# A fused attention and two-layer-pair kernel: the last product's first four row chunks in the seven-product form, the other two added plain

## The chip, the cores and the metric

The kernel runs on one core of one Trainium2 chip. The metric is device time in microseconds (us) of one execution; lower is better. The engines are TensorE (PE, with its weight loads shown as PEld), VectorE (DVE), ScalarE (ACT), GpSimd (POOL) and SyncE (SP), which issues all DMAs here.

## The reference

Linear attention with a normalised output, a softplus layer pair, and a max-of-three layer pair, all in float32:

```python
kv = einsum('bhsd,bhse->bhde', k, v); out = einsum('bhsd,bhde->bhse', q, kv)
x = (out / sqrt(mean(out*out, -1) + 1e-6) * g_norm)      # 4608 tokens x 512
g = softplus(x @ w_in)                                   # 512 -> 2048
x = g @ w_out                                            # 2048 -> 512
h = maximum(maximum(x @ w1, x @ w2), x @ w3)             # 512 -> 768
y = h @ w2_out                                           # 768 -> 512
```

## The kernel before

The 4608 tokens are worked in five passes of two halves each (464 tokens to a half, 448 in the last pass). Activations lie with features on the partitions, so a feature dimension is counted in row chunks of 128.

**The seven-product form.** A product of a 2x2 block of weights with a 2x2 block of activations (two row chunks by two token halves) is done with seven block products and some sums instead of eight block products (Winograd's form of Strassen's method). `run_group` issues the seven in the order 1, 5, 6, 2, 7, 4, 3 at the places of `SLOT`; `combine` (or `combine32` in pass 0) makes the seven sums of activations, `sums_of_weights` those of the weights, and products accumulate in three kinds of PSUM bank (`BANK`: X and Y with two buffers, W with one). After products 1, 6 and 7 the bank is copied out, because later products go on adding to it. The products x @ w_in (8 groups, "H"), g @ w_out (8, "X") and x @ w1..w3 (9, "2") have this form; the last, h @ w2_out, has not: `out_part` runs it as 6 row chunks by 4 output chunks by 2 halves.

**Precision.** In pass 0 a block is one float32 matmul (`L318`, `L696`; two instructions each). In the passes 1 to 4 each operand is split into a high and a low part of the type float32r, and a block is three matmuls (`mm3`, L127 to L129). A split is a cast on ACT (L111) and a subtraction on POOL or DVE (L117).

**Weights.** In pass 0 the raw weights are loaded, converted (`to_f32`), summed and, for groups below `LATE` = 19, split into four units per group (`make_unit`), which are kept in DRAM for the later passes (`keep`). For the groups from 19 on, and for the last product's weights ("oa" for row chunks 0 to 3, "ob" for 4 and 5), only the float32 sums are kept; pass 1 loads them (`load_sums`, tile `st`, two buffers), splits and keeps them (`make_later`). The passes 2 to 4 load ready units (`load_unit`). Three units of a group hold two blocks (tile `u`, four buffers, or `ux`); the fourth, for product 3, holds one (tile `u3`, `U3_BUFS` = 2), and so do the "ob" units.

**Order.** Every step is entered with `at(t, ...)`, t being counted in places of one block product (six matmuls in passes 1 to 4). The steps are issued in order of t, and the framework's scheduler then orders each engine's instructions by this priority among those that it holds ready, gives out the tile buffers as they come free, and adds all waits. On the chip each engine runs its list in order. `attention_beside` puts the next pass's attention (`load_kv`, `kv_mm`, `kv_evict`, `out_mm`) beside the end of a pass, and from pass 2 on `start["H0"]` lies `SHARED` = 12 places before the pass's base, so that its first group overlaps the last product of the pass before. The group 16 begins at `base2`, the last product at `base3 = base2 + 63`.

Of the kernel before, what the change touches and what calls it, by code (L numbers as in the profile page):

```python
# [15 lines left out]
P = 128  # L16
# [16 lines left out]
LATE = 19  # L33
# [7 lines left out]
def kernel(  # L41
# [157 lines left out]
    def raw_of(g):  # L199
        if g < 8:  # L200
            return [w_in[2 * g + i] for i in range(2)]
        if g < 16:
            return [w_out[2 * (g - 8) + i] for i in range(2)]
        f, j = divmod(g - 16, 3)
        return [w123[2 * f + i, j] for i in range(2)]
# [61 lines left out]
    def convert_out(j, i):  # L267

        if i == 0:
            sw["o", j] = pools["raw"].tile([P, 3, 512], F32, tag="sw", bufs=3, name="swo")  # L270
        to_f32(raws.pop(("o", j, i)), sw["o", j][:, i])
# [288 lines left out]
    def run_pass(pas, base):  # L560
# [5 lines left out]
        def weights_at(t, g, stretch=1):  # L566
            if pas == 0:
# [83 lines left out]
        def h2_done(fp, j, w, src):  # L651
# [9 lines left out]
            if j == 2:  # L661
                src = mx.pop(key)
                at_ = 2 * fp + w // 20, w % 10 - 1
                if pas == 0:
                    hh[at_] = src
                else:
                    hi, lo = gc_tile("hh", N, F32R), gc_tile("hl", N, F32R)
                    split(nc.scalar, src, hi, lo, nc.gpsimd)
                    hh[at_] = (hi, lo)

# [9 lines left out]
        if pas + 1 < NPASS:  # L680
            attention_beside(pas + 1, start["X30"], base2)
# [4 lines left out]
        acc = {}  # L686

        def out_part(e, t, part):
            if part == 0:
                acc[e, t] = psum("at" if e > 1 else ("at", "X")[e], "oacc")[:, 0:N]  # L690
            if pas == 0:
                w = sw["o", e // 2][:, 2 * part or e % 2]
                for k in range((4, 2)[part]):
                    f = 4 * part + k
                    o = k + (part and 2 * (e % 2))
                    nc.tensor.matmul(acc[e, t], w[:, o * P:(o + 1) * P], hh[f, t], start=f == 0,  # L696
                                     stop=f == NF2 - 1)
            else:
                u = units[pas, (("oa", "ob")[part], e)]
            for k in range(0 if pas == 0 else (4, 2)[part]):  # L700
                f = 4 * part + k
                xh, xl = hh[f, t]
                cs = slice(k * P, (k + 1) * P)
                if part == 0:
                    wh, wl = u[:, 0, cs], u[:, 1, cs]
                else:
                    wh, wl = u[:, 0, cs], u[:, 0, slice(256 + k * P, 256 + (k + 1) * P)]
                mm3(acc[e, t], wh, wl, xh, xl, f == 0, f == NF2 - 1)
            if part == 1:
                o = ctile("osb", N)  # L710
                if t:
                    nc.vector.tensor_copy(o, acc[e, t])
                else:
                    nc.scalar.copy(o, acc[e, t])
                a = TOK[pas] + t * N
                nc.sync.dma_start(out=out[e * P:(e + 1) * P, a:a + N], in_=o)

        t = base3 + 2.05
        if pas == 0:
            for j in range(2):  # L720
                tj = t + 12 * j
                for i in range(3):
                    src = w2_out[2 * j + i if i < 2 else KC + j]
                    jobs.append((tj - 12 + 2 * i, ("o", j, i), src, convert_out, (j, i)))
                at(tj + 1, keep_sums, ("o", j))
        parts = [(e, part) for part in range(2) for e in range(2)]
        parts += [(e, part) for e in (2, 3) for part in range(2)]
        for i, (e, part) in enumerate(parts):
            if pas == 1:
                c0, n = ((512 * (e % 2), 512), (1024 + 256 * (e % 2), 256))[part]  # L730
                make_later(t, (("oa", "ob")[part], e), 2 - part, ("o", e // 2), c0, n)
            elif pas:
                own = i == 0
                at(t - (6 if own else LEAD), load_unit, pas, (("oa", "ob")[part], e), 2 - part, own)
            for h in range(2):
                at(t, out_part, e, h, part)
                t += (2, 1)[part] * (1 if i < 4 or pas in (0, NPASS - 1) else 1.6)
        if 0 < pas < NPASS - 1:
            t -= 7.2
        return t - 0.05  # L740
# [57 lines left out]
def _laid_out(inputs):  # L798
# [10 lines left out]
    def cols(w):  # L809
# [9 lines left out]
        [w2[:, :, 0:4].reshape(KC, P, DM),  # L819
# [39 lines left out]
```

## Time and profile before

| | us |
|---|---|
| median of 3 runs | 1489.62 (1486.07 to 1490.92) |
| the profiled execution, its own time | 1490.04 |
| its span in the profile | 1488.2 |
| PE, PEld busy | 1427.3, 1129.2 |
| DVE, ACT, POOL busy | 933.3, 834.5, 674.9 |

The span runs from the first to the last instruction; 1.8 us of the execution's time lie outside it. Busy times of the engines overlap each other. A matmul's busy time is modelled and longer than its place in the stream (0.37 us for a 464-column one that follows the one before after 0.21 us), so idle time before an instruction says more than the busy share.

### The profile page before, as it was taken

The page shows a single profiled execution, that of the slowest core. Times are in us where ns is not written, and L with a number is a line of the kernel's source. Part 1 is how long each engine was busy: PE and PEld are TensorE (multiplying, and loading weights), DVE is VectorE, ACT ScalarE, POOL GpSimd, SP SyncE. Part 2 cuts the span into 40 slices and gives each one's busy share as a digit, 9 for nine tenths or more (in the row PEclk, how much of TensorE's full clock was granted, in tenths as well). Part 3 has the DMA queues.
Part 4 walks back from the last instruction along what each step waited for, and adds up shares of the span by engine and source line. Part 5 has one row for each costly group of instructions (what it writes and reads, how often), then busy time and mean ns, then how long its engine had stood idle before and what let it go on. Part 6 is the DMA issues. An engine that isn't in the chain of part 4 may idle for free.

```text
span 1488.2 us, 18882 instructions
## 1 busy us (share of the span) xinstructions
PE 1427.3 (96%) x6164; PEld 1129.2 (76%) x6164; DVE 933.3 (63%) x1476; ACT 834.5 (56%) x1625; POOL 674.9 (45%) x613
## 2 busy tenths in 40 slices
PE   6898999999999999999999999999999999999999
PEld 4344444555588888778889898888888888898898
DVE  5787887689365676773666556355675554567432
ACT  5676453564197636764866366387636636864321
POOL 3587776643243454451545434434444452534311
PEclk9999999999999999999999999999999999999999
DMA  7657667964366775766566676566665656666572
GB/s 271 250 196 271 213 222 275 324 205 152 120 200 202 220 243 198 263 218 217 186 216 218 228 259 195 168 197 213 217 213 191 201 179 206 203 219 211 188 220 97
DMA packets 107954, 315.56 MB, mean 212 GB/s; under 512 B 12113, under 2 KB 23633, under 8 KB 107857
## 3 DMA queue, kind: packets, MB, share of 16 engines
q1 hardware_dynamic: 107856, 314.36, 63.8%
q8 instruction: 50, 0.82, 0.2%
q14 instruction: 48, 0.39, 0.1%
HBM read 248.78 MB, written 65.54 MB: 211 GB/s over the span
## 4 chain that ended last, share of the span: by engine, by line
PE 72%; DVE 9%; ACT 8%; DMA 4%; issue 4%; POOL 3%; SPq 0%; ACTq 0%; POOLq 0%; DVEq 0%
PE Xo L128 3%; PE Xo L127 3%; PE Xo L318 3%; PE Xo L129 3%; PE Xx L127 3%; PE Xx L129 3%; PE Xx L128 3%; PE Xh L127 3%; PE Xh L129 3%; PE Xh L128 3%; PE oacc L129 3%; PE oacc L128 3%; PE oacc L127 3%; PE oacc L696 3%; PE kvps L412 2%
## 5 line engine op out<-in xcount | busy, mean ns | idle before, releaser
L117 POOL TENSOR_TENSOR lo<-e,hi 128x464 fp32r<-128x464 f32 (+1 forms) x160 | 190.6, 1224 | 201.3 <-ACT hi L111 165.2
L123 POOL TENSOR_TENSOR e<-e 128x464 f32<-128x464 f32 (+1 forms) x40 | 48.2, 1204 | 190.1 <-DVE t L123 172.6
L111 ACT COPY m<-Xo 128x464 f32<-128x464 f32 (+1 forms) x135 | 72.6, 542 | 88.8 <-PE Xo L129 76.9
L117 POOL TENSOR_TENSOR hl<-m,hh 128x464 fp32r<-128x464 f32 (+1 forms) x48 | 58.5, 1222 | 106.2 <-ACT hh L111 106.2
L111 ACT CAST hi<-e 128x464 fp32r<-128x464 f32 (+1 forms) x160 | 87.5, 576 | 21.7 <-PE Yx L128 17.5
L111 ACT CAST hi<-t 128x464 fp32r<-128x464 f32 (+1 forms) x96 | 52.0, 543 | 84.5 <-DVE e L123 38.2
L375 DVE SCALAR_TENSOR_TENSOR e<-h,e 128x464 f32<-128x464 f32 (+1 forms) x80 | 69.5, 871 | 47.1 <-ACT e L374 46.5
L120 DVE TENSOR_TENSOR x<-x,Xx 128x464 f32<-128x464 f32 (+1 forms) x120 | 75.2, 628 | 31.5 <-PE Xx L129 30.1
L374 ACT ACTIVATE e<-e 128x464 f32<-128x464 f32 (+1 forms) x160 | 92.8, 588 | 2.7
L373 ACT ACTIVATE e<-e 128x464 f32<-128x464 f32 (+1 forms) x160 | 92.8, 588 | 2.4
L117 POOL TENSOR_TENSOR u<-sw,u 128x512 fp32r<-128x512 f32 (+1 forms) x76 | 87.9, 1186 | 10.4 <-ACT u L111 10.4
L127 PE MATMUL Xo<-hi,u 128*128 128x464 f32 (+1 forms) x228 | 87.9, 385 | 3.9 <-ACT m L111 3.6
L128 PE MATMUL Xo<-lo,u 128*128 128x464 f32 (+1 forms) x228 | 86.6, 380 | 0.2 <-DVE lo L117 0.2
L220 ACT ACTIVATE cv<-raw 128x512 f32<-128x512 f32 x56 | 35.8, 640 | 90.2 <-DVE sw L231 49.3
L129 PE MATMUL Xo<-hi,u 128*128 128x464 f32 (+1 forms) x228 | 86.1, 378 | 0.0
L123 POOL TENSOR_TENSOR sw<-sw 128x256 f32<-128x256 f32 x75 | 57.1, 762 | 62.0 <-DVE sw L231 45.2
L519 POOL TENSOR_TENSOR og<-og,r 128x464 f32<-128x464 f32 (+1 forms) x32 | 41.0, 1280 | 90.1 <-DVE r L509 82.0
L127 PE MATMUL Xh<-hi,u 128*128 128x464 f32 (+1 forms) x194 | 73.3, 378 | 4.7 <-ACT h L111 4.3
L129 PE MATMUL Xh<-hi,u 128*128 128x464 f32 (+1 forms) x194 | 71.9, 371 | 0.0
L127 PE MATMUL Xx<-hi,u 128*128 128x464 f32 (+1 forms) x192 | 71.8, 374 | 0.0
L128 PE MATMUL Xh<-lo,u 128*128 128x464 f32 (+1 forms) x194 | 71.8, 370 | 0.0
L111 ACT COPY h<-Xh 128x464 f32<-128x464 f32 (+1 forms) x108 | 57.6, 536 | 25.0 <-PE Xh L129 21.4
(229 smaller groups left out, 4330.3 us busy)
## 6 DMA issues: line engine op xcount, KB each, us to landing
u<-wd SPq DMA_DIRECT2D x198, 512.0 KB, 4.3
ux<-wd SPq DMA_DIRECT2D x96, 512.0 KB, 3.4
wd<-u SPq DMA_DIRECT2D x79, 512.0 KB, 3.0
u<-wd SPq DMA_DIRECT2D x106, 256.0 KB, 3.7
raw<-in_w_out_dram SPq DMA_DIRECT2D x22, 512.0 KB, 4.2
k<-in_kp_dram SPq DMA_DIRECT2D x32, 320.0 KB, 5.0
v<-in_vp_dram SPq DMA_DIRECT2D x32, 320.0 KB, 5.3
raw<-in_w_dram SPq DMA_DIRECT2D x18, 512.0 KB, 3.9
```

The lines of the kernel that those rows point to most:

```text
L111: nc.scalar.copy(hi, src)
L117: eng_lo.tensor_tensor(out=lo, in0=src, in1=hi.bitcast(F32), op=ALU.subtract)
L120: eng.tensor_tensor(out=o, in0=a, in1=b, op=ALU.add)
L123: eng.tensor_tensor(out=o, in0=a, in1=b, op=ALU.subtract)
L127: nc.tensor.matmul(acc, wh, xh, start=first, stop=False, skip_group_check=on)
L128: nc.tensor.matmul(acc, wh, xl, start=False, stop=False, skip_group_check=on)
L129: nc.tensor.matmul(acc, wl, xh, start=False, stop=last, skip_group_check=on)
L318: nc.tensor.matmul(acc, w[:, c * P:(c + 1) * P], rhs[m, c], start=first and c == 0, stop=c == 1, skip_group_check=not first)
L373: nc.scalar.activation(e, e, AF.Exp, scale=-1.0)
L374: nc.scalar.activation(e, e, AF.Ln, bias=1.0)
L375: nc.vector.scalar_tensor_tensor(out=e, in0=src, scalar=0.0, in1=e, op0=ALU.max, op1=ALU.add)
L696: nc.tensor.matmul(acc[e, t], w[:, o * P:(o + 1) * P], hh[f, t], start=f == 0, stop=f == NF2 - 1)
```

## The change

The row chunks 0 to 3 of h become two groups more (25 and 26, one for two output chunks each) in the seven-product form; their activations' sums are made by `combine_h` in the middle of the "2" groups. The row chunks 4 and 5 are added plain (`rest`) into the same banks before these are read out; for the fourth block, 22, into a bank of its own. `LATE` is no longer a bound but a list of ten groups that are spread over the X groups, the "2" groups and the new ones; the subtraction of every other unit made in pass 1 goes to POOL instead of DVE. The next pass's first kv products move from the middle of the X groups (X30) to six places before `base2`, two places apart instead of three. The last product is counted with 24 places, of which two are waiting.

```diff
-LATE = 19
+LATE = (9, 11, 13, 15, 17, 19, 21, 23, 25, 26)
...
     def split_unit(key, size):
         u = units[1, key] = unit_tile(size, 1)
         src = st.pop(key)
-        if key[0] == "oa":
-            split(nc.scalar, src, u[:, 0], u[:, 1], nc.vector)
-        else:
-            split(nc.scalar, src.rearrange("p (i n) -> p i n", i=size), u[:, :, 0:256], u[:, :, 256:512], nc.vector)
+        split(nc.scalar, src.rearrange("p (i n) -> p i n", i=size), u[:, :, 0:256], u[:, :, 256:512],
+              nc.gpsimd if key[1] % 2 else nc.vector)
...
-    def attention_beside(pas, t_kv, t0):
+    def attention_beside(pas, t0):
...
-        for t, tt in ((0, t_kv), (1, t0 + 16)):
+        for t, tt, d in ((0, t0 - 6, 2), (1, t0 + 16, 3)):
...
-                    at(tt + 3 * p - (10 if p < 2 else 5.85), load_kv, b, p)
-                    at(tt + 3 * p + 0.1, kv_mm, b, p)
-                at(tt + (9.2 if t == 0 else 10.35), kv_evict, b)
+                    at(tt + d * p - (10 if p < 2 else 2 * d - 0.15), load_kv, b, p)
+                    at(tt + d * p + 0.1, kv_mm, b, p)
+                at(tt + 3 * d + (0.2 if t == 0 else 1.35), kv_evict, b)
...
-                if g >= LATE:
+                if g in LATE:
                     at(t + 1, keep_sums, g)
-                for k in range(4 if g < LATE else 0):
+                for k in range(0 if g in LATE else 4):
                     at(t + 1.6 * k, make_unit, g, k)
-            elif pas == 1 and g >= LATE:
+            elif pas == 1 and g in LATE:
...
-            if j == 2:
+            if j == 2 and fp == 2:
...
-                    hi, lo = gc_tile("hh", N, F32R), gc_tile("hl", N, F32R)
+                    hi, lo = ge_tile(pas, "hh", N).bitcast(F32R), ge_tile(pas, "hl", N).bitcast(F32R)
                     split(nc.scalar, src, hi, lo, nc.gpsimd)
...
+        def combine_h(c, steps):
+            tiles = [mx[c, w] for w in TILES]
+            if pas == 0:
+                combine32(gc_tile, ho, c, tiles)
+            else:
+                combine(gc_tile, ho, c, tiles, steps, "W")
+
+        for c in range(2):
+            for s in range(6 if pas else 1):
+                at(base2 + 21 * c + 28 + 1.2 * s, combine_h, c, (s,))
...
-            attention_beside(pas + 1, start["X30"], base2)
+            attention_beside(pas + 1, base2)
...
+        def rest(E, i, t, acc, first=False):
+            e = 2 * E + i
+            for k in range(2):
+                if pas == 0:
+                    o = (2 * i + k) * P
+                    nc.tensor.matmul(acc, sw["o"][:, E, o:o + P], hh[k, t], start=first and k == 0,
+                                     stop=k == 1, skip_group_check=not first)
                 else:
+                    u = units[pas, ("ob", e)][:, 0]
+                    mm3(acc, u[:, k * P:(k + 1) * P], u[:, 256 + k * P:256 + (k + 1) * P], *hh[k, t],
+                        first and k == 0, k == 1, not first)
+
+        def last_group(E, t0, stretch):
...
+            def after(m, b):
+                bank.update(b)
+                if m in (1, 6, 7):
+                    w = {1: 11, 6: 12, 7: 22}[m]
+                    c[w] = ctile(f"o{w}", N)
+                    nc.scalar.copy(c[w], b["X"])
+                if m == 7:
+                    add(nc.vector, c[22], c[22], b["Y"])
+
+            def finish(w):
+                i, t = w // 20, w % 10 - 1
+                acc = psum("at", "oacc")[:, 0:N] if w == 22 else bank[{11: "W", 21: "X", 12: "Y"}[w]]
+                rest(E, i, t, acc, w == 22)
+                if w == 21:
+                    c[21] = ctile("o21", N)
+                    nc.scalar.copy(c[21], acc)
                 else:
+                    add(nc.vector, c[w], c[w], acc)
+                store(i, t, c[w])
+
+            weights_at(t0, 25 + E, stretch)
+            run_group(t0, pas, 25 + E, ho, after, stretch)
+            for w, m, d in ((11, 2, 2.5), (21, 4, 0.5), (12, 3, 0.4), (22, 3, 0.8)):
+                at(t0 + stretch * SLOT[m] + d, finish, w)
+            for i in range(2):
+                key = ("ob", 2 * E + i)
+                t = t0 + stretch * SLOT[2] + 2.5 + 2 * i
+                if pas == 1:
+                    make_later(t, key, 1, "o", 512 * E + 256 * i, 256)
+                elif pas:
+                    at(t - LEAD, load_unit, pas, key, 1)
...
+        last_group(0, base3, 1.25)
+        last_group(1, base3 + 9, 1.25)
+        return base3 + 24
```

The removed function `out_part` and its calls are in the kernel above.

## Rows read from the trace of the kernel before

**Rows 1.** The profile page: span, busy time (share) and instructions of each engine.
```profile
span 1488.2 us, 18882 instructions
PE 1427.3 (96%) x6164; PEld 1129.2 (76%) x6164; DVE 933.3 (63%) x1476; ACT 834.5 (56%) x1625; POOL 674.9 (45%) x613
```

**Rows 2.** Windows: busy us per engine by stretch, granted clock, DMA share, GB/s; five passes.
```profile
0.00:404.00 404.00, 367.34 (x1063) 188.60 (x1064) 304.22 (x478) 211.53 (x411) 233.38 (x249) 0.98 0.65 226
404.00:680.00 276.00, 265.71 (x1253) 231.81 (x1252) 184.61 (x282) 175.43 (x343) 121.21 (x98) 0.99 0.68 223
680.00:956.00 276.00, 272.94 (x1338) 242.04 (x1337) 157.74 (x252) 163.10 (x315) 119.39 (x98) 0.99 0.65 211
956.00:1232.00 276.00, 272.81 (x1310) 241.37 (x1309) 157.32 (x252) 161.90 (x315) 119.05 (x98) 0.99 0.62 200
1232.00:1488.00 256.00, 248.47 (x1208) 225.35 (x1206) 129.39 (x213) 122.55 (x242) 81.88 (x70) 1.00 0.61 192
```

**Rows 3.** Chain that ended last, start and us: matmuls of passes 0, 1 and 4.
```profile
372.54 31.13 PE oacc L696 x80
...
406.39 0.21 PE Xh L128
...
1471.12 0.20 PE oacc L127
```

**Rows 4.** Waits of PE: total us, times, longest; the ones that bear on this.
```profile
PE Xx L318 <- DVE x L120: 5.7, 4, 1.9
PE Xo L127 <- ACT hi L111: 5.7, 4, 1.8
PE Xo L127 <- ACT m L111: 3.6, 2, 3.2
PE Yo L127 <- DVE m L660: 2.2, 3, 1.4
PE Xo L128 <- DVE lo L117: 2.0, 5, 0.5
```

**Rows 5.** Windows: stretches at the lower clock (PE, PEld, DVE, ACT, POOL, PEclk, DMA, GB/s).
```profile
557.60:561.20 3.60, 3.49 (x9) 2.60 (x10) 2.95 (x6) 2.28 (x5) 3.53 (x4) 0.53 0.10 14
653.00:657.00 4.00, 3.69 (x10) 3.23 (x11) 4.00 (x9) 1.47 (x4) 1.27 (x2) 0.57 0.59 183
841.00:844.60 3.60, 3.52 (x10) 2.53 (x9) 2.13 (x4) 2.64 (x6) 3.55 (x4) 0.53 0.43 146
1117.50:1121.10 3.60, 3.60 (x10) 2.39 (x10) 2.34 (x4) 2.64 (x6) 3.55 (x4) 0.53 0.40 146
```

**Rows 6.** Windows: pass 0's middle, and pass 1's "2" groups before the last product.
```profile
100.00:150.00 50.00, 44.09 (x110) 20.04 (x109) 38.90 (x60) 31.92 (x63) 38.15 (x40) 1.00 0.77 268
150.00:200.00 50.00, 46.05 (x118) 21.83 (x117) 41.37 (x66) 28.30 (x55) 34.32 (x36) 1.00 0.68 231
200.00:250.00 50.00, 45.11 (x133) 22.75 (x132) 41.21 (x66) 16.29 (x31) 37.58 (x38) 0.97 0.74 262
300.00:350.00 50.00, 50.00 (x154) 27.02 (x152) 44.30 (x70) 29.05 (x55) 23.67 (x25) 1.00 0.55 190
600.00:653.00 53.00, 48.12 (x220) 40.27 (x218) 41.21 (x61) 36.47 (x72) 20.86 (x17) 1.00 0.72 247
```

**Rows 7.** Chain, pass 0 between 170 and 196 us, and pass 1 before 653 us.
```profile
173.68 5.16 DMA wd<-u
178.83 0.60 ACT u L111
...
184.19 6.08 DMA wd<-u
...
646.59 5.04 DMA st<-ws
...
652.81 0.45 ACT m L111
653.31 0.70 PE Xo L127
```

**Rows 8.** Timeline of PE at a boundary from the X groups to the "2" groups.
```profile
554.48 0.36 PE L129 MATMUL o<-qh,kvl 128*128 128x448 f32 x1
...
556.33 0.48 PE L127 MATMUL Xo<-hi,ux 128*128 128x464 f32 x1 [1.25 <-ACT hi L111]
...
557.71 0.68 PE L128 MATMUL Xo<-lo,ux 128*128 128x464 f32 x1 [0.45 <-DVE lo L117]
```

**Rows 9.** Chain: one kv product of the next pass's attention.
```profile
529.44 1.11 PE kvps L412 x10
```

**Rows 10.** DMA issues: count, KB each, median us to landing; passes 1 to 4, then from 1440.
```profile
u<-wd SPq DMA_DIRECT2D x104, 256.0 KB, 3.7
v<-in_vp_dram SPq DMA_DIRECT2D x14, 320.0 KB, 5.0
st<-ws SPq DMA_DIRECT2D x10, 128.0 KB, 2.1
...
u<-wd SPq DMA_DIRECT2D x3, 512.0 KB, 4.4
u<-wd SPq DMA_DIRECT2D x5, 256.0 KB, 2.9
```

**Rows 11.** SP's waits in 404 to 680 us, and the subtractions of pass 1's units (ns min/median/max).
```profile
SPq L181 <- DVE u L117: 48.8, 26, 6.2
...
L117 DVE TENSOR_TENSOR u<-st,u x32: 412/692/1714, 571.5 to 673.6; 128x512 fp32r<-128x512 f32 x22, 128x256 fp32r<-128x256 f32 x10
```

**Rows 12.** The page: units' subtractions in pass 0 on POOL; activations' subtractions on POOL.
```profile
L117 POOL TENSOR_TENSOR u<-sw,u 128x512 fp32r<-128x512 f32 (+1 forms) x76 | 87.9, 1186 | 10.4 <-ACT u L111 10.4
L117 POOL TENSOR_TENSOR hl<-m,hh 128x464 fp32r<-128x464 f32 (+1 forms) x48 | 58.5, 1222 | 106.2 <-ACT hh L111 106.2
```

**Rows 13.** Windows: a stretch of passes 2 and 3 with "2" groups and last product.
```profile
840.00:980.00 140.00, 139.91 (x692) 125.03 (x693) 69.01 (x108) 73.95 (x141) 55.91 (x46) 0.99 0.62 204
```

**Rows 14.** Timeline: the end of the program.
```profile
1484.55 0.62 DVE L712 COPY osb<-oacc 128x448 f32<-128x448 f32 x1 [6.67 <-PE oacc L129]
```

More of the change, by code (lines that the diff above doesn't have):

```diff
@@ L203, in raw_of @@
             return [w_out[2 * (g - 8) + i] for i in range(2)]
+        if g > 24:
+            return [w2_out[2 * (g - 25) + i] for i in range(2)]
         f, j = divmod(g - 16, 3)
@@ L265, in make_unit, with convert_out @@
         keep((g, k), u)
[L267 to L271, printed above, removed]
+    def convert_out(j):
+        if j == 0:
+            sw["o"] = pools["raw"].tile([P, 2, 512], F32, tag="sw", bufs=3, name="swo")
+        to_f32(raws.pop(("o", j)), sw["o"][:, j])
     STEPS = ((1,), (5, 6), (2,), (7,), (4,), (3,))
@@ L660, in h2_done @@
                 nc.vector.tensor_tensor(out=mx[key], in0=mx[key], in1=src, op=ALU.max)
-            if j == 2:
+            if j == 2 and fp == 2:
                 src = mx.pop(key)
-                at_ = 2 * fp + w // 20, w % 10 - 1
+                at_ = w // 20, w % 10 - 1
                 if pas == 0:
@@ L666, in h2_done @@
                 else:
-                    hi, lo = gc_tile("hh", N, F32R), gc_tile("hl", N, F32R)
+                    hi, lo = ge_tile(pas, "hh", N).bitcast(F32R), ge_tile(pas, "hl", N).bitcast(F32R)
                     split(nc.scalar, src, hi, lo, nc.gpsimd)
                     hh[at_] = (hi, lo)
+        ho = {}
+        def combine_h(c, steps):
[7 more added lines that the diff above has]
+                at(base2 + 21 * c + 28 + 1.2 * s, combine_h, c, (s,))
         for k in range(9):
@@ L680, in run_pass @@
         if pas + 1 < NPASS:
-            attention_beside(pas + 1, start["X30"], base2)
+            attention_beside(pas + 1, base2)
             for s, ms in enumerate(STEPS):
                 at(base3 - 2 + SLOT[ms[-1]] + 0.5, combine_x, pas + 1, (s,))
[L686 to L705, printed above, removed]
-                else:
[L707 to L712, printed above, removed]
-                else:
-                    nc.scalar.copy(o, acc[e, t])
-                a = TOK[pas] + t * N
-                nc.sync.dma_start(out=out[e * P:(e + 1) * P, a:a + N], in_=o)
@@ L718, in run_pass @@
-        t = base3 + 2.05
+        def rest(E, i, t, acc, first=False):
[5 more added lines that the diff above has]
+                                     stop=k == 1, skip_group_check=not first)
+                else:
+                    u = units[pas, ("ob", e)][:, 0]
+                    mm3(acc, u[:, k * P:(k + 1) * P], u[:, 256 + k * P:256 + (k + 1) * P], *hh[k, t],
+                        first and k == 0, k == 1, not first)
@@ new lines, in last_group, with store @@
+        def last_group(E, t0, stretch):
+            c, bank = {}, {}
+            def store(i, t, o):
+                e, a = 2 * E + i, TOK[pas] + t * N
+                nc.sync.dma_start(out=out[e * P:(e + 1) * P, a:a + N], in_=o)
+            def after(m, b):
[13 more added lines that the diff above has]
+                    nc.scalar.copy(c[21], acc)
+                else:
+                    add(nc.vector, c[w], c[w], acc)
[11 more added lines that the diff above has]
+                    at(t - LEAD, load_unit, pas, key, 1)
@@ L719, in run_pass @@
         if pas == 0:
             for j in range(2):
[L721 to L737, printed above, removed]
@@ L738, in run_pass @@
-        if 0 < pas < NPASS - 1:
-            t -= 7.2
-        return t - 0.05
+                jobs.append((base3 + 5 + 2 * j, ("o", j), w2_out[KC + j], convert_out, (j,)))
+            at(base3 + 9, keep_sums, "o")
+        last_group(0, base3, 1.25)
+        last_group(1, base3 + 9, 1.25)
+        return base3 + 24
     nc.scalar.preload_act_table_set("natural_log_exp_and_others")
@@ L818, in _laid_out @@
     w2 = np.concatenate(
-        [w2[:, :, 0:4].reshape(KC, P, DM),
+        [w2[:, :, (0, 2, 1, 3)].reshape(KC, P, DM),
          w2[:, :, 4:6].reshape(2, 2, P, 256).transpose(0, 2, 1, 3).reshape(2, P, DM)]
```

## The prediction

> **What bounds the kernel now.** I read the page first: PE is busy for 96% of the span, DVE for 63%, ACT 56%, POOL 45% [rows 1]. By passes [rows 2], the reader is to see two kinds of stage. In the passes 2 to 4 PE is idle for 3 to 7.5 us of 256 to 276, so there only less work for PE, or an idle stretch of PE that I can name, changes the time. In pass 0 PE is idle for 36.7 us, and in pass 1 for 10.3 us; there the other engines decide some stretches. The waits of PE [rows 4] say which: in pass 0 it waits for DVE's and ACT's sums of X; at four boundaries from the X groups to the "2" groups for the first sums (hi, then lo); in pass 1 for copies and maxima (m) that stand behind something on ACT and DVE. Windows with the lower clock come last [rows 5]: four stretches at about half (0.53 to 0.57), so at 1.2 instead of 2.4 GHz, each behind a gap; one such stretch of 3.4 to 3.6 us loses some 1.7 us.
>
> **Work removed from PE.** Before, a pass runs 6 x 4 x 2 = 48 blocks in the last product. After, two groups of 7 products x 2 row chunks = 28 blocks, and 2 row chunks x 4 output chunks x 2 halves = 16 plain ones: 44. In the passes 1 to 4 that is 12 matmuls less. One takes 0.21 us at 464 columns, and 0.20 at 448 [rows 3]: 3 x 12 x 0.21 + 12 x 0.20 = 10.0 us. In pass 0 four float32 blocks go, two instructions each; 80 instructions took 31.13 us [rows 3], so 0.389 each: 3.1 us. Together 13.1 us, all on the path if nothing new makes PE wait.
>
> **The boundary before the "2" groups (kv moved).** In the passes 1 to 3 PE runs out after the last X product but for a few attention matmuls (o), waits 1.25 us for a cast and 0.45 us for a subtraction [rows 8], and then loses 1.7 us at the lower clock (the stretches at 557, 841 and 1117 us in [rows 5]); the four boundaries waited 5.7 + 2.0 us [rows 4]. After, o cannot run there, because its kv is not yet evicted; four kv products of 1.11 us each [rows 9] can. But a kv buffer pair is loaded again only when a product two places of p earlier is done, and v takes 5.0 us to land [rows 10]; four places of PE with one kv product between are 4 x 1.26 + 1.11 = 6.2 us, so the third and fourth come just in time. Bounds: all idle and low clock of three passes gone, about 3 x (1.7 + 1.7) = -10.2 us; or a late v, +1 us a pass, +3. I take -3 us: nearer to one us of filling a pass, with the clock left open.
>
> **LATE spread.** Pass 0 makes 17 x 4 = 68 units instead of 76, and of the twelve groups from X00 to X31 four leave the stretch where PE is idle for 14.8 us of 150 [rows 6]. There DVE is busy for some 80%, and the chain passes through the keeping of units (5.16 and 6.08 us of transfer before ACT may write the next, [rows 7]). Three of the late groups (20, 22, 24) now make units where PE has no idle time and POOL is half free (23.7 of 50 us; 12 units x 1.19 us are added [rows 6, 12]). Bounds 0 and -14.8; I take a third, -5 us.
>
> In pass 1, before, all 32 late units come between 570 and 673 us, and their loads wait 48.8 us on SP for DVE to free a buffer of st [rows 11]. One load of 5.04 us held ACT, behind which the copy m stood, for which PE waited 3.2 us [rows 4, 7], with 1.7 us of low clock behind it; with the waits for m on DVE (2.2) that is some 7 us. After, 44 units are made, but 16 of them in the X groups, 16 in the "2" groups, and 12 in the last product, where each is wanted sooner. I take -3 us; bounds -8 (all gone) and +6 (twice the 3.2 us stall in the last product).
>
> Of the 44, 22 subtractions go to POOL. Rows: a DVE subtraction of a unit takes 692 ns in the median, and up to 1714 [rows 11], 1.02 us more. The Trainium skill (SBUF — State Buffer, "Who interferes with whom") says that a DVE instruction with two SBUF inputs and a GpSimd instruction that reads SBUF exclude each other for the whole instruction; by that rule, the trace's two lengths are free and blocked ones, and POOL's new work would block DVE. By the median the move frees 22 x 0.69 = 15 us of DVE in pass 1; if each POOL operation held DVE up once, it would cost 22 x 1.02 = 22 us of DVE instead, with 91 us of DVE idle to take it [rows 2]. I leave the sum at -3 and price the other below.
>
> **What is added beside PE.** Each `combine_h` makes 7 splits instead of 4 and 4 sums: per pass 6 more casts, 4 more POOL operations of 1.2 us and 10 more of DVE of about 0.65; reading out adds 4 copies and 4 additions. In the passes 2 and 3 DVE is busy for 69 and POOL for 56 of 140 us [rows 13], so PE's own work hides them. The one place on the path: the sum for product 6 sits in the single W bank, which the groups' product 2 also wants, eight times. I take +1 us, bounds 0 and +5.
>
> **The single-block units.** `u3` has two buffers. In a new group three such units are wanted at once: "ob" for output chunk 0 (blocks 11 and 12), for chunk 1 (21 and 22), and that of product 3, which block 12 needs first. So product 3's load can't start before block 22 is finished, the next group's "ob" not before product 3 is done, and so on down the end of the pass. In pass 4 nothing follows that could fill. In places of 6 x 0.203 = 1.22 us from the last product's first: 14 places of other work (two are the last group 24's), then block 22 until 15; a load of 256 KB landed in 2.9 us there [rows 10], with some 0.4 for the issue 3.3 us = 2.7 places; product 3 at 17.7, block 12 until 19.7; the next "ob", asked for at 18.7, at 21.4; its blocks 11, 21, 22 until 24.4; the second product 3 at 27.1, done with block 12 at 29.1. Without waits it is 24. So +5.1 places = +6.2 us at the end of pass 4. Bounds: 2.1 us a load (the shortest of [rows 10]) gives 3.8; 4.4 us, and one low-clock stretch behind the last gap, 12. After the last matmul nothing changes: a DVE addition stands where the copy of 0.62 us did [rows 14].
>
> In the passes 1 to 3 the same chain runs beside the next pass's first group, 42 matmuls x 0.21 = 8.8 us that PE can take instead. I take +1 us a pass, +3; bounds 0 and 3 x (6.2 + 1.7) = 24.
>
> **Sum.** -13.1 - 3 - 5 - 3 + 1 + 6.2 + 3 = -13.9 us from 1490.04, the profiled execution's own time (1488.2 of it the span), which lies 0.4 above the median 1489.62: 1476 us.
>
> **The rivals.** *More comes of it:* the kv products close the boundaries and the low clock goes (-8), pass 0 gains half of its idle time (-8), pass 1 -5, and the ends cost 4 in all, W nothing: 1490 - 13.1 - 8 - 8 - 5 + 4 = 1460. For it: PE's idle stretches are few, and each has its filler; against: the just-in-time v. *Nothing comes of the spreading and moving:* 1490 - 13.1 + 1 + 6.2 + 3 = 1487. For it: DVE at 80% in pass 0 keeps every conversion. *DVE blocked by POOL:* a third of the 22 us meets DVE where it is busy for 41 of 53 us [rows 6], +7.5 instead of gaining: 1476 + 7.5 = 1483. *Slower:* the chain of the single-block units is not filled in the passes 1 to 3 either, since the next group's product 5 waits for the Y bank and its product 2 for the W bank, which blocks 12 and 11 hold until their units land: 4 x (6.2 + 1.7) = 31.6 us at -13.1 - 3 - 5 + 1, so 1501. It decides from (13.1 + 3 + 5 - 1) / 4 = 5.0 us a pass.
>
> **How the numbers follow.** The forecast has 0.60, with its own range 1468 to 1484; more 0.17; nothing but PE's work 0.11; DVE blocked 0.05; slower 0.07. The range 1462 to 1487 leaves out the slower case, about half of the 1460 case and a little of the 1487 one. A change of 0.3% (4.5 us, 1485.1 and 1494.1) is about what a measurement of this kernel tells from none. Faster: nearly all of 0.60, 0.17 and most of 0.05: 0.80; same: the 0.11 and the rest, 0.13; slower 0.07.
>
> **What would show it.** 132 matmuls of the last product in each of the passes 1 to 4, at 0.21 us; PE idle in 100 to 250 us down from 14.8 to about 10; no PE wait of 3 us at pass 1's end; the boundary's waits near 0.7 us a pass; at the end of pass 4 three PE gaps of some 2 to 3 us, each ended by a 256 KB load of u. The prediction is wrong if these gaps stand at the end of every pass, or if pass 4's end has none, or if kv's matmuls wait for v.

## The result, and the profile after

The change made the kernel slower by half a per cent: 1497.34 us in the median of 6 runs (1495.98 to 1499.5), against 1489.9 for the kernel before, measured again beside it (6 runs, 1486.07 to 1493.64). The ratio is 1.0053, with a 95% interval of 1.0035 to 1.0072. The profiled execution took 1498.40 us, its span 1496.6, so 8.4 more than before in either [rows 1].

The head of the page of the changed kernel, as in [rows 1]:

```profile
span 1496.6 us, 18992 instructions
PE 1422.3 (95%) x6108; PEld 1120.7 (75%) x6108; DVE 967.5 (65%) x1530; ACT 855.0 (57%) x1673; POOL 718.8 (48%) x655
```

PE runs 56 matmuls less, exactly the 4 x 12 + 8 that were counted. Its busy time falls by 5.0 us only, and the mean granted clock fell with it, from 0.991 to 0.987; its idle time grows from 60.9 to 74.3 us. So the work did go, and waits took more than its place. The waits of PE (engine, line, releaser: total us, times, longest) say which, beside [rows 4]:

```profile
PE kvps L412 <- DMA v<-in_vp_dram: 10.8, 4, 5.3
PE Yo L127 <- DMA u<-wd: 7.1, 5, 3.0
...
PE Yo L318 <- POOL sw L120: 4.3, 1, 4.3
...
PE Yo L127 <- DVE m L661: 3.0, 2, 2.8
...
PE Xh L127 <- ACT o L734: 2.4, 1, 2.4
...
PE Xx L318 <- DVE x L120: 2.3, 4, 1.1
PE Xx L318 <- POOL t L123: 2.0, 1, 2.0
...
PE Xo L127 <- ACT hi L111: 1.8, 1, 1.8
```

The reader is to see that pass 0's waits for DVE's sums of X went down (5.7 to 2.3 us, with 2.0 new for such a sum on POOL), and so did the boundary's for the cast (5.7 to 1.8), as the change meant them to. The upper five lines hold what came in their place: the load of v (5.3 us of it, once at the start, stood before as well; 5.5 are new), the loads of the single-block units, a sum of weights on POOL, and at pass 1's end a maximum and an eviction.

To find where the 8.4 us came from, I laid the two PE timelines beside each other, stage by stage, marking the stages by the groups of matmuls (a group begins with its first matmul). The difference of each stage, after less before, in us:

| stage | pass 0 | pass 1 | pass 2 | pass 3 | pass 4 |
|---|---|---|---|---|---|
| H groups and X groups | -5.7, with the first four "2" groups (+1.9 at the start, then -7.6) | +0.8 | +0.2 | -0.1 | 0.0 |
| boundary to the "2" groups | in the line above | +2.6 | -3.2 | -3.2 | +1.6 |
| "2" groups | +5.7 (5th to 9th) | -3.3 | +1.4 | +0.2 | +0.1 |
| end: from group 24 to the third H group of the next pass | +3.6 | +1.7 | +1.0 | 0.0 | +5.0 |

The ends, where the product lies that the change makes cheaper, are each as long as before or longer. The 1.9 us at the start are no more than scatter: kernels with the changed kernel's code up to there begin their first H group between 47.6 and 49.4 us.

**Pass 0.** Windows after (us, then busy us of PE, PEld, DVE, ACT and POOL with counts, granted clock, DMA share, GB/s): the stretch of the X groups, and two later ones.

```profile
100.00:250.00 150.00, 140.36 (x371) 67.55 (x370) 124.65 (x198) 71.80 (x137) 99.13 (x104) 0.99 0.67 233
293.00:344.00 51.00, 47.75 (x144) 25.14 (x143) 42.03 (x67) 28.97 (x56) 31.83 (x31) 0.97 0.64 225
344.00:416.00 72.00, 67.50 (x189) 36.03 (x189) 42.79 (x70) 24.89 (x48) 27.48 (x28) 0.98 0.50 181
```

In the X groups PE's idle time falls from 14.8 us [rows 6] to 9.6, of which 2.5 are a new wait for v, since the moved kv stands there now. But between 293 and 344 us, where PE had no idle time before [rows 6], it now has 3.3 us. Behind that the end of the pass loses 4.3 us in one wait. The chain that ended last (start, us, what), and the PE instruction at its end on the timeline:

```profile
377.14 2.27 POOL lo L117 x2
379.41 0.69 POOL sw L123
380.10 1.12 POOL lo L117
381.22 0.69 POOL sw L120
381.91 0.04 issue
381.95 1.11 PE Yo L318 x2
```
```profile
381.95 1.89 PE L318 MATMUL Yo<-t,sw 128*128 128x464 f32 x3 [4.32 <-POOL sw L120]
```

The sums of the last product's weights (`sw`) are new work of POOL, four for each of two groups. They stand in POOL's order between subtractions of the next pass's activations (`lo`), and PE waits until the last of them is through.

**Pass 1.** The chain before its end:

```profile
648.44 1.60 POOL og L519
650.04 1.14 POOL lo L117
651.18 1.79 POOL u L117
652.98 2.41 DMA st<-ws
...
655.46 0.41 ACT u L111
...
655.95 0.42 DVE u L117
656.38 0.56 DVE m L661
...
656.98 0.48 PE Yo L127
```

A unit's subtraction that went to POOL stands there behind POOL's own work (`og`, `lo`). Only when it is done is a buffer of `st` free for the next load. That load holds ACT's cast, then DVE's subtraction, and behind that the maximum `m`, for which PE waits 2.8 us. It is the chain of [rows 7] again, with POOL at its head.

**Pass 4.** Its end, on PE's timeline: three gaps, each ended by a load of u.

```profile
1481.31 0.48 PE L127 MATMUL Wo<-hh,u 128*128 128x448 f32 x1 [1.15 <-DMA u<-wd]
...
1482.95 0.47 PE L127 MATMUL Xo<-hh,u 128*128 128x448 f32 x1 [0.16 <-DMA u<-wd]
...
1488.64 0.64 PE L127 MATMUL Yo<-hi,u 128*128 128x448 f32 x1 [2.98 <-DMA u<-wd]
```

### The profile page after: what moved, and what is told of

It is laid out like the page before. It is cut to its first block, busy times and chain, and to the rows that moved or that the text cites. A ratio compares the mean times of both kernels' runs of the same rounds, so it can differ in the third digit from the quotient of the medians.

```text
span 1496.6 us, 18992 instructions
## 1 busy us (share of the span) xinstructions
PE 1422.3 (95%) x6108; PEld 1120.7 (75%) x6108; DVE 967.5 (65%) x1530; ACT 855.0 (57%) x1673; POOL 718.8 (48%) x655
## 4 chain that ended last, share of the span: by engine, by line
PE 65%; DVE 6%; ACT 5%; DMA 5%; POOL 4%; issue 3%; SPq 0%; POOLq 0%; DVEq 0%; ACTq 0%
PE Xo L128 4%; PE Xo L127 4%; PE Xo L129 4%; PE Xx L127 3%; PE Xx L129 3%; PE Xx L128 3%; PE Xh L127 3%; PE Xh L129 3%; PE Xh L128 3%; PE Yo L127 2%; PE Yo L129 2%; PE Yo L128 2%; PE Xo L318 2%; POOL lo L117 2%; DMA u<-wd 2%
## 5 line engine op out<-in xcount | busy, mean ns | idle before, releaser
L111 ACT CAST hi<-t 128x464 fp32r<-128x464 f32 (+1 forms) x112 | 60.9, 544 | 93.5 <-DVE e L123 37.7
L127 PE MATMUL Xo<-hi,u 128*128 128x464 f32 (+1 forms) x276 | 103.8, 376 | 0.9 <-ACT o L724 0.9
L129 PE MATMUL Xo<-hi,u 128*128 128x464 f32 (+1 forms) x276 | 103.0, 373 | 0.0
L128 PE MATMUL Xo<-lo,u 128*128 128x464 f32 (+1 forms) x276 | 102.9, 373 | 0.0
L375 DVE SCALAR_TENSOR_TENSOR e<-h,e 128x464 f32<-128x464 f32 (+1 forms) x80 | 65.8, 826 | 47.4 <-ACT e L374 43.4
L123 POOL TENSOR_TENSOR sw<-sw 128x256 f32<-128x256 f32 x81 | 61.6, 760 | 72.1 <-DVE sw L231 39.6
L117 DVE TENSOR_TENSOR lo<-t,hi 128x464 fp32r<-128x464 f32 (+1 forms) x112 | 70.3, 630 | 20.0 <-ACT hi L111 18.7
L117 POOL TENSOR_TENSOR u<-sw,u 128x512 fp32r<-128x512 f32 (+1 forms) x68 | 78.7, 1186 | 8.4 <-ACT u L111 8.4
L127 PE MATMUL Xh<-hi,u 128*128 128x464 f32 (+1 forms) x194 | 73.6, 380 | 5.4 <-ACT h L111 5.3
L127 PE MATMUL Xx<-hi,u 128*128 128x464 f32 (+1 forms) x200 | 74.9, 374 | 0.9 <-DVE x L120 0.9
L129 PE MATMUL Xx<-hi,u 128*128 128x464 f32 (+1 forms) x200 | 74.1, 371 | 0.0
L128 PE MATMUL Xx<-lo,u 128*128 128x464 f32 (+1 forms) x200 | 74.0, 370 | 0.0
```

Of the source, the lines that this page charges most:

```text
L111: nc.scalar.copy(hi, src)
L117: eng_lo.tensor_tensor(out=lo, in0=src, in1=hi.bitcast(F32), op=ALU.subtract)
L123: eng.tensor_tensor(out=o, in0=a, in1=b, op=ALU.subtract)
L127: nc.tensor.matmul(acc, wh, xh, start=first, stop=False, skip_group_check=on)
L128: nc.tensor.matmul(acc, wh, xl, start=False, stop=False, skip_group_check=on)
L129: nc.tensor.matmul(acc, wl, xh, start=False, stop=last, skip_group_check=on)
```

## The experiments

Each kernel is compared with the kernel before on the same chip, as a ratio with its 95% interval in brackets. Stages and spans are those of one profiled execution each. Theory: five things cost time, and each can be taken away by itself: the two buffers of `u3`, kv's place in passes 0 and 1, the sums of weights on POOL, the late units' new places, and the subtractions on POOL.

**A third buffer for the single-block units** (`ge` gives one of its own for the room).

```
-U_BUFS, U3_BUFS, GE_BUFS = 4, 2, 14
+U_BUFS, U3_BUFS, GE_BUFS = 4, 3, 13
```

> The changed kernel with a third buffer for the single-block units (and one ge buffer less, 13 for 14, to make room; the engines' order does not change by that alone). Theory: the chain of single-block units holds the ends of passes 1 to 4; the gaps ended by a 256 KB load of u (changed kernel: 7.1 + 1.1 us by PE's waits, with up to 3 us more of low clock) go, pass 4 from its first "2" group to the end falls from 117.6 to about 110 us, and the whole time falls by 7 to 11 us, to about 1488. Rival: these gaps only stand in for work of ACT, DVE and POOL on the read-out that is not done yet; then other waits take their place and the time falls by less than 2 us.

Measured: 1479.26 us, ratio 0.9942 [0.9928, 0.9956], 18.3 us under the changed kernel by the spans and 16.5 by the ratios (1.0053 - 0.9942), well above what was expected. All waits for `u<-wd` are gone. Windows of the ends of the passes 2 and 3, of the changed kernel and then of this one:

```profile
950.00:975.00 25.00, 22.48 (x105) 19.03 (x104) 7.90 (x13) 7.84 (x15) 3.36 (x3) 1.00 0.68 214
1225.00:1250.00 25.00, 23.42 (x111) 20.03 (x110) 8.66 (x13) 7.88 (x15) 1.16 (x1) 1.00 0.72 224
```
```profile
950.00:975.00 25.00, 25.00 (x119) 21.86 (x118) 8.79 (x14) 8.56 (x16) 1.20 (x1) 1.00 0.80 246
1225.00:1250.00 25.00, 25.00 (x123) 22.64 (x122) 12.26 (x22) 16.90 (x33) 2.32 (x2) 1.00 0.76 240
```

The ends took 64.8, 59.0, 57.5 and 45.5 us (passes 1 to 4) in the changed kernel and take 61.0, 55.9, 55.3 and 37.9 here. So the chain of two buffers cost 3.8 + 3.2 + 2.2 + 7.5 = 16.7 us; 1.5 more of the 18.3 lie at pass 4's boundary, where the clock was lower in the changed kernel (last section). Against before (63.1, 58.1, 57.4, 40.5), the form with its units in time gives 2.1 to 2.5 us an end, which is what 12 matmuls less are worth.

**The same buffers in the kernel before**, as a control.

```
-U_BUFS, U3_BUFS, GE_BUFS = 4, 2, 14
+U_BUFS, U3_BUFS, GE_BUFS = 4, 3, 13
```

> The kernel before with a third buffer for the single-block units (and 13 ge buffers for 14), nothing else. Theory: before, no two such units were wanted at once beside product 3's, so the third buffer gives nothing: within 2 us of before. Rival: the third buffer helps by itself, by loading product 3's units earlier everywhere; then 4 us or more faster, and what it gave the changed kernel is not the chain's price.

Measured: 1487.33 us, 0.9995 [0.9986, 1.0004]. The buffer is worth nothing clear of noise without the new form; what it gains there is the form's. One stage of this trace is a warning: pass 1's end is 59.5 us, 3.6 shorter than in the trace of the kernel before, with a wait for m of 1.2 us instead of 3.2, behind a load of `st` of 2.69 us instead of 5.04 [rows 7]. The medians being equal, one execution can differ that much there, so what the end of pass 1 gains against the one trace of before is less sure than the other ends.

**kv back in its old place**, the rest as in the changed kernel.

```
-        for t, tt, d in ((0, t0 - 6, 2), (1, t0 + 16, 3)):
+        for t, tt, d in ((0, t_kv, 3), (1, t0 + 16, 3)):
...
-            attention_beside(pas + 1, base2)
+            attention_beside(pas + 1, start["X30"], base2)
```

> The changed kernel with the next pass's first kv products back where they were (middle of the X groups, three places apart). Theory: moving them helped by 3.2 us each in passes 2 and 3 (the boundary's wait and low clock are gone there) and cost 2.6 us in pass 1 and some 4 us in pass 0's "2" groups, where PE now waits for v (2.7 and 2.5 us, each with a stretch at the low clock); put back, the boundary at pass 1 gains some 2 us, those at passes 2 and 3 lose 3 each, pass 0 gains 4: within 2 us of the changed kernel's 1497. Rival: the just-in-time v is what made the change slow; then the time falls by 6 us or more.

Measured: 1497.11 us, 1.0063 [1.0044, 1.0081], the same as the changed kernel. By stages two halves cancel: it is 4.8 us ahead at the end of pass 0 (1.4 of it from the program's start, before any moved product), wins 2.6 at pass 1's boundary, and loses 2.9 and 2.5 at those of the passes 2 and 3 and 2.0 at pass 2's end. Pass 1's end is as long as in the changed kernel (65.3 us; 64.8 there).

**The sums of weights of the last product on DVE**, the rest as in the changed kernel.

```
-        sub(nc.gpsimd, s3, a11, s1)
+        eng = nc.vector if g > 24 else nc.gpsimd
+        sub(eng, s3, a11, s1)
...
```

> The changed kernel with the sums of weights of the two new groups (25 and 26, pass 0) made on DVE instead of POOL. Theory: PE's wait of 4.3 us at the end of pass 0 (and 1.7 us of low clock behind it) is for sums that stand on POOL behind the next pass's subtractions; on DVE, idle then, they are ready some 4 us earlier: 4 to 6 us less, about 1492. Rival: the late load and conversion of the raw weights sets the time, and POOL is only the last link; then DVE's sums save at most 2 us.

Measured: 1494.36 us, 1.0035 [1.0017, 1.0052]. The wait of 4.3 us is gone from PE's waits, and the end of pass 0 goes from 70.2 to 66.1 us, -4.1. The whole time shows less of it: 2.7 us by the ratios, with intervals that overlap, so the price of this wait rests on the stage. The end is still only 0.5 us under that of before (66.6): waits of 1.3 and 0.8 us for the conversion (`swo`) and sums (`sw`) of the last product's weights, now on DVE, remain.

**The kernel before with the late units spread**, and nothing else.

```
-LATE = 19
+LATE = (9, 11, 13, 15, 17, 19, 21, 23)
...
-                if g >= LATE:
+                if g in LATE:
```

> The kernel before with nothing changed but the list of late groups: 9, 11, 13, 15, 17, 19, 21, 23 in place of 19 to 24. Theory: pass 0's X groups gain 7 to 8 us, as in the changed kernel, its "2" groups lose some of it (units for 20, 22 and 24), pass 1's "2" groups gain 3 us: 5 to 8 us faster than before, about 1483. Rival: what the X groups gain is given back in full in the "2" groups, since DVE's conversions set pass 0's pace throughout: within 2 us of before.

Measured: 1478.29 us, 0.9938 [0.9922, 0.9953]. This part alone (the spread kernel, from here on) is worth 0.6%, some 9 us. Pass 0 gains 8.7 us from its first H group to the fifth "2" group and gives 3.7 back behind it. Pass 1 gains 8.1, most of it at its end (63.1 to 58.4 us), where the wait of 3.2 us for m [rows 4] and the low clock behind it are gone. Of these 4.7 us, 3.6 came in the control with the third buffer too, so the traces do not show how much of them is the spreading's.

**The form and the third buffer**, with the late units in one block and kv in its old place.

```
-U_BUFS, U3_BUFS, GE_BUFS = 4, 2, 14
-LATE = (9, 11, 13, 15, 17, 19, 21, 23, 25, 26)
+U_BUFS, U3_BUFS, GE_BUFS = 4, 3, 13
+LATE = (19, 20, 21, 22, 23, 24, 25, 26)
...
+        for t, tt, d in ((0, t_kv, 3), (1, t0 + 16, 3)):
```

> The seven-product form alone, with a third buffer for the single-block units: late groups as before (19 to 24, with the new 25 and 26), kv products as before. Theory: the form is worth 2.1 to 2.5 us at each of the four pass ends once the units can land, loses 3.6 at the end of pass 0 (sums on POOL) and some 2 in pass 1, where twelve more units are made at the end: 1484 to 1487, so 2 to 5 us faster than before. Rival: the sums of h and the read-out cost on ACT, DVE and POOL what PE saves: 1489 or more.

POOL's share of the subtractions and its sums of weights stay in this kernel. Measured: 1490.17 us, 1.0015 [1.0007, 1.0024]. The forecast was missed; the rival was nearer. With its units in time the form still gains nothing as a whole. The last three ends save 2.2, 2.2 and 2.5 us and pass 1's 1.5, but PE is 5.2 us late by pass 1's second X group, most of it from pass 0's "2" groups and end, and loses 1.8 more in pass 2's "2" groups. Its profile still has the wait for the sums of weights:

```profile
PE Yo L318 <- POOL sw L120: 3.9, 1, 3.9
```

**All subtractions of pass 1's units on DVE**, the rest as in the changed kernel.

```
         split(nc.scalar, src..., u[:, :, 0:256], u[:, :, 256:512],
-              nc.gpsimd if key[1] % 2 else nc.vector)
+              nc.vector)
```

> The changed kernel with all of pass 1's unit subtractions on DVE, as before (the change put every other one on POOL). Theory: in pass 1 v is late not for its own transfer but because SP, in order, stands before it at the keeping of a unit whose subtraction waits on POOL (SP waits 12.5 us for POOL between 540 and 566 us in the changed kernel); on DVE the unit is done earlier, PE's wait of 2.7 us for v and the low clock behind it go, and the time falls by 3 to 5 us, to about 1493. Rival 1: v is late because four places are too few; then nothing changes at that boundary. Rival 2: POOL's share relieved DVE, busy with 22 more subtractions now, and pass 1 becomes slower by some us.

Measured: 1487.12 us, 0.9996 [0.9984, 1.0008], 9.8 us under the changed kernel by the spans and 8.5 by the ratios, twice what was expected: pass 1's boundary gains 4.7 us, its end 5.7. The subtractions between 404 and 700 us (ns min/median/max), in the changed kernel and then here:

```profile
L117 DVE TENSOR_TENSOR u<-st,u x22: 417/692/1652, 443.7 to 685.2; 128x512 fp32r<-128x512 f32 x20, 128x256 fp32r<-128x256 f32 x2
L117 POOL TENSOR_TENSOR u<-st,u x22: 731/1146/1813, 450.6 to 696.0; 128x256 fp32r<-128x256 f32 x12, 128x512 fp32r<-128x512 f32 x10
```
```profile
L117 DVE TENSOR_TENSOR u<-st,u x44: 414/693/1705, 444.2 to 687.1; 128x512 fp32r<-128x512 f32 x30, 128x256 fp32r<-128x256 f32 x14
```

DVE is held up by POOL in both kernels. In the second, timelines of DVE and of POOL:

```profile
619.17 1.42 DVE L117 TENSOR_TENSOR u<-st,u 128x512 fp32r<-128x512 f32 x1
...
618.84 1.20 POOL L117 TENSOR_TENSOR lo<-m,hi 128x464 fp32r<-128x464 f32 x1 [1.18 <-ACT hi L111]
```

The subtraction on DVE begins while POOL is at work until 620.04 us, and ends 0.55 us behind that. So it goes with all of them: 8 of the 22 on DVE in the changed kernel, and 17 of the 44 here, begin while an operation of POOL runs, and just these are over 0.1 us longer than the shortest of their shape. That is the rule that I had weighed in the prediction (the Trainium skill, SBUF — State Buffer, "Who interferes with whom"), and these rows agree with it. But it is not what the move cost. POOL's other work holds DVE up as well, and by the excess over the shortest operation of each kind in these traces, DVE lost some 20 us in pass 1 of the changed kernel (32 long operations) and some 25 us here (39). What differs is the order of things behind POOL. SP's issues in the changed kernel at pass 1's boundary, and here:

```profile
550.47 0.32 SPq L165 DMA_DIRECT2D wd<-u  x1
...
551.31 0.44 SPq L403 DMA_DIRECT2D v<-in_vp_dram  x1
```
```profile
548.58 0.42 SPq L403 DMA_DIRECT2D v<-in_vp_dram  x1
```

In the changed kernel the load of v is issued 2.7 us later. It stands on SP behind the keeping of a unit (`wd<-u`), and SP waits there for POOL's half of that unit (SP's waits, 540 to 566 us):

```profile
SPq L165 <- POOL u L117: 12.5, 3, 4.7
```

PE's wait for v at this boundary is 2.7 us in the changed kernel, 1.2 here. From the second X group of the third pair to the third "2" group the changed kernel takes 56.8 us, this one 52.1, and so does the spread kernel (52.2) with kv in its old place; so no run shows that the moved kv gains anything at this one.

**Every other subtraction on POOL in the kernel before**, with the late units spread (the fifth kernel above) and the last product plain.

```
-            split(nc.scalar, src, u[:, 0], u[:, 1], nc.vector)
+            split(nc.scalar, src, u[:, 0], u[:, 1], nc.gpsimd if key[1] % 2 else nc.vector)
...
```

> The kernel before with the spread list of late groups (1478.3) and every other unit subtraction of pass 1 on POOL, last product plain, kv where it was. Theory: SP keeps units in order, so a keep that waits for POOL, whose queue holds longer operations, delays the loads behind it whatever the last product's form: 3 to 8 us slower than with the list alone, 1481 to 1486, most of it at pass 1's end. Rival: POOL is late only because the new form gives it more work there; then within 2 us of 1478.

Measured: 1479.21 us, 0.9944 [0.993, 0.9958], as without POOL's share (1478.29). The rival held: by itself the move costs little. In the traces pass 1, which alone has it, takes 278.4 us against 276.6 (from its third H group to the next pass's), 1.6 of the difference at the boundary. And yet SP waits for POOL there nearly as long as in the changed kernel (its waits, 404 to 700 us, in the changed kernel and then here):

```profile
SPq L165 <- POOL u L117: 39.0, 12, 5.1
...
SPq L181 <- POOL u L117: 20.7, 9, 5.9
```
```profile
SPq L165 <- POOL u L117: 35.1, 12, 5.2
...
SPq L181 <- POOL u L117: 16.9, 6, 5.8
```

So SP's wait is not the price in itself. The reading that fits is that it becomes one where something that PE wants soon is queued behind it: v at the boundary, where kv was moved to, and the last product's units, which the new form wants closer together. That it is these two was not tested one by one.

**The third buffer and all subtractions on DVE**, the rest as in the changed kernel.

```
+U_BUFS, U3_BUFS, GE_BUFS = 4, 3, 13
...
+              nc.vector)
```

> The changed kernel with two repairs only: the third buffer for the single-block units and all of pass 1's unit subtractions on DVE. Theory: they act at different waits (passes 2 to 4's ends; pass 1), but overlap at pass 1's end, where the third buffer alone gained 3.8 us and DVE alone 5.7: 18 + 10 less 2 to 4, so about 1471 to 1473. Rival: both gains are one (one late chain in pass 1 that either repair breaks); then about 1478.

Measured: 1474.3 us, 0.9905 [0.9892, 0.9919]: 24.2 us under the changed kernel by the spans (22.1 by the ratios), where the two alone make 18.3 + 9.8 = 28.1. What they share lies mostly at pass 1's end (58.3 us here; 61.0 and 59.1 with the one or the other). So two lines turn a loss of 0.5% into a gain of 1%.

**A first version put together:** third buffer, sums on DVE, kv moved only beside the passes 2 and 3.

```
+U_BUFS, U3_BUFS, GE_BUFS = 4, 3, 13
...
+        eng = nc.vector if g > 24 else nc.gpsimd
...
+        for t, tt, d in ((0, t0 - 6, 2) if pas > 2 else (0, t_kv, 3), (1, t0 + 16, 3)):
```

> The changed kernel with all three repairs: a third buffer for the single-block units, the sums of groups 25 and 26 on DVE, and the moved kv products only beside passes 2 and 3 (beside 0 and 1 where they were). Theory: the repairs add up, since they act in different stretches: from 1479.3 with the third buffer, 4 us less at the end of pass 0, 3 to 4 in pass 0's "2" groups, 3 at pass 1's boundary: 1468 to 1471. Rival: what one repair frees in passes 0 and 1 is lost again to the next wait there, since DVE is busy for 80% of pass 0: 1476 or more.

Measured: 1470.31 us, 0.9876 [0.9864, 0.9889], as expected.

**The same without the new form:** the kernel before with the late units spread and kv moved beside the passes 2 and 3.

```
+LATE = (9, 11, 13, 15, 17, 19, 21, 23)
...
+        for t, tt, d in ((0, t0 - 6, 2) if pas > 2 else (0, t_kv, 3), (1, t0 + 16, 3)):
```

> The kernel before with the spread list of late groups and the moved kv products beside passes 2 and 3 only; the last product stays plain. Theory: the 10 us of the spread list and some 3 us at each of two boundaries add up: 1470 to 1474. The difference to the kernel with all three repairs is what the seven-product form is worth: 2 to 4 us. Rival: the gain at the boundaries comes of the form (its sums leave PE's list differently); then within 2 us of the 1478.3 of the spread list alone.

Measured: 1473.79 us, 0.9901 [0.9888, 0.9914]. Most of the gain needs no seven-product form; the form, with its third buffer and its sums on DVE, adds 0.25%, some 3.7 us (0.9901 to 0.9876), though the version with the form still has POOL's share of the subtractions.

**The best version:** the first one with all subtractions on DVE too, and kv moved in all passes but pass 0.

```
+        for t, tt, d in ((0, t0 - 6, 2) if pas > 1 else (0, t_kv, 3), (1, t0 + 16, 3)):
...
+              nc.vector)
```

> The kernel with all three repairs, and pass 1's unit subtractions on DVE, so that the kv products can stand at their new place beside pass 1 too (only pass 0 keeps the old one). Theory: some 3 us more at pass 1's boundary: 1467. Rival: DVE's 22 more subtractions cost pass 1 as much: 1470 or more.

Measured: 1466.11 us, 0.9858 [0.9843, 0.9873]: 1.4% under the kernel before, and by the ratios (0.9858 / 1.0053) 1.9% under the changed one. Two things changed together from the first version, so the total doesn't say which paid. By stages, pass 1's boundary is 2.0 us shorter and pass 1's end 3.2 (57.0 for 60.2); kv beside pass 1 stood in its old place in the first version, which points to POOL's share as costing time at that end even with the third buffer and without the moved kv.

## Why the prediction was wrong, point by point

It said 1476 and faster; it was 1497.34 and slower. Its own sum said -13.9 us from the profiled execution, and +8.4 came: 22.3 us too low.

- **Work removed from PE: right as work, wrong as "all on the path if nothing new makes PE wait".** The matmuls are 56 fewer, as counted, and 2.1 to 2.5 us an end came out once the units were in time. In pass 0 something new did make PE wait. I priced the sums and splits of the activations, but not the eight sums of the new weights on POOL, which come behind the next pass's subtractions. That cost the 4.1 us that moving them to DVE gave back. And of the 3.1 us of work in pass 0 only 0.5 showed even then, with 2.1 us of waits for the same weights left.
- **The single-block units: the mechanism was right, the size was off.** The term was 6.2 for pass 4 and, for the others, "I take +1 us a pass, +3", 9.2 in all. Measured were 7.5 and 3.8 + 3.2 + 2.2, together 16.7. In pass 4 three gaps stood as announced, if of 1.15, 0.16 and 2.98 us instead of 2 to 3 each, and the lower clock came behind the last (0.60 from 1488.6 to 1492.9 us), which I had put into the bound only. In the passes 1 to 3 the next pass's first group filled more than half of the gaps, but not nearly all of them as I had taken. The slower rival's 5.0 us a pass was not reached, and its time of 1501 was near for other reasons besides its own.
- **"I leave the sum at -3" for the 22 subtractions on POOL: the step that failed most.** Taking them back gave 9.8 us. I looked for a loss in the lengths of DVE's operations. They do get longer beside POOL's, but DVE lost no more by it with POOL's share than without (some 20 us against 25), so my rival "DVE blocked by POOL" was not what happened either. I did not ask who queues behind POOL: the buffer of `st`, SP's next issues, v, and the units. Most of the loss needs the new form beside it: in the spread kernel without form and moved kv the same move cost pass 1 1.7 us, and putting kv back in the changed kernel left pass 1's end as long as it was. At pass 1's end the rows show the chain. How much of the 4.7 us at the boundary is v, whose wait differs by 1.5 us, was not separated further.
- **LATE spread: about right for pass 0, by two errors that cancel.** The idle time of pass 0's X groups fell to 9.6 us, where about 10 had been written, and the stage gained more than I took. But "Three of the late groups (20, 22, 24) now make units where PE has no idle time" was priced at nothing, and the later "2" groups gave part of it back. Net, from the first H group to group 24, the spread kernel gained 8.7 - 3.7 = 5.0 us and the changed kernel with kv put back 10.4 - 5.1 = 5.3, where I had 5. The changed kernel itself has only 7.6 - 5.7 = 1.9; the rest is the moved kv's price in pass 0 (below). Pass 1 could gain as I said, by up to 8 us in the spread kernel's trace (with the doubt at pass 1's end told there); POOL's share hid it.
- **What is added beside PE: "+1 us" for the W bank was right in size, by luck.** The "2" groups of the passes 2 to 4 are 1.4, 0.2 and 0.1 us longer, but no wait of PE for that bank stands in these passes' rows. In pass 2, 0.9 is a wait for a subtraction of the attention on POOL (`sl`).
- **The boundary: right in the passes 2 and 3, better than taken** (-3.2 us each, at the bound's good end). In pass 1 it came out at +2.6, as v was late there. That is the sign that I had named as "if kv's matmuls wait for v", and without POOL's share the boundary is at -2.0, as it is in the spread kernel with kv in its old place. In pass 0, which I had left out, the moved kv costs 3.4 us (5.3 - 1.9): PE waits 2.5 us for v there.

Chain and POOL's share together cost 24.2 us (measured with both undone; 22.1 by the ratios) where 9.2 was priced: 15.0. With 4.1 for the sums of weights and 3.4 for the moved kv in pass 0 that is 22.5, where 22.3 are to be explained. That it closes so well is in part chance, for differences of both signs are left over: 2.6 us of pass 0's work that did not come, the boundaries of the passes 2 and 3 (better), 1.9 us at the start of pass 0, and 1.6 at pass 4's boundary, where the clock was lower.

The step behind most of them is one: for each added or moved operation I asked how long it takes and whether its engine has room, and only for the single-block units what has to be finished before it may start.

## What to carry to other kernels

When a form needs its operands in smaller pieces and sooner, count the buffers of each size that are wanted at once. Here one more buffer of the small units was worth 16 to 18 us, more than all the matmuls that the form saves. When an operation moves to an idle engine, its own length can be the least of it, as here: follow what that engine's order puts ahead of it, and what waits behind its result, on the queue that issues the loads above all. And judge each part of a compound change by itself: here the spreading of the late units alone was worth 0.6%, and it would have been lost with the rest. Put a stage's loss down to a part only when the kernel without that part has been read at the same stage: pass 0's loss looked like the spreading's and was the moved kv's.

## What the hardware showed that I had not expected

The granted clock differed behind gaps of the same kind. At pass 4's boundary PE waits in both kernels for the same cast, behind the same matmuls of an X group at full clock. PE's timeline there, before and then after:

```profile
1377.22 0.47 PE L127 MATMUL Xo<-hi,ux 128*128 128x448 f32 x1 [1.83 <-ACT hi L111]
```
```profile
1378.99 0.47 PE L127 MATMUL Xo<-hi,ux 128*128 128x448 f32 x1 [1.80 <-ACT hi L111]
```

The 8 us from 1377 us read 1.00 before. After, the window from 1379 us reads 0.57, close to the lower level of 1.2 GHz, and the stage is 1.6 us longer:

```profile
1377.00:1385.00 8.00, 6.97 (x27) 4.90 (x28) 4.97 (x8) 4.42 (x10) 7.91 (x7) 1.00 0.39 116
```
```profile
1379.00:1387.00 8.00, 7.83 (x21) 6.01 (x22) 4.58 (x7) 3.83 (x8) 7.91 (x7) 0.57 0.26 93
```

What made the difference, the rows don't show; it stays open. Comparing one trace with another, 1.6 us at such a place can be the clock's. At the end of pass 4 the gap of 2.98 us is followed by nine matmuls of 0.37 to 0.64 us on the chain, where 0.20 is the rule (start, us, what):

```profile
1488.64 0.64 PE Yo L127
1489.28 0.37 PE Yo L128
1489.65 0.37 PE Yo L129
```
